# Second scores of one batch and first scores of the next in one run of matmuls, in shared banks

## The chip, the core and the metric

The kernel runs on one core of a Trainium2 chip. A core has a matrix engine (TensorE, in the profile PE, with its weight loads as PEld), three engines for the rest (VectorE or DVE, ScalarE or ACT, GpSimd or POOL), and queues that start transfers between the chip's main memory and the on-chip memory (SP and POOL start nearly all of them here). Matmuls write to eight accumulator banks (PSUM) of 128 partitions x 512 fp32 columns; DVE and ACT read them out. Every engine works through its own list of instructions in order, and waits on counters that other engines raise. The metric is the device time of one execution, in microseconds; before the change it is 241.86 us (median of 3 runs, 241.26 to 241.97).

## The reference

Eight batches, eight heads, 576 positions, head dimension 64, 32 "packed" queries `p` for each head. First attention: the packed queries attend to the keys. Second attention: the 576 queries attend to the 32 packed results, which are keys and values at once. Then a feed-forward layer with a squared relu on the 4608 positions.

```python
def sm_attn(qq, kk, vv):
    s = scale * np.matmul(qq, kk.transpose(0, 1, 3, 2))
    s = s - np.max(s, axis=-1, keepdims=True)
    a = np.exp(s)
    a = a / (np.sum(a, axis=-1, keepdims=True) + 1e-09)
    return np.matmul(a, vv)
p_packed = sm_attn(p, k, v)
out = sm_attn(q, p_packed, p_packed)
x = out.transpose(0, 2, 1, 3).reshape(B * S, H * D)
h = x @ w_in
r = np.maximum(h, 0.0)
return ((r * r) @ w_out).astype(np.float32)   # w_in 512 x 2048, w_out 2048 x 512
```

## The kernel before

Matmul operands are bf16, accumulators fp32. The eight heads of a batch are two "quads" of four (`NQ` is 2, `QH` is 4); all work of a batch `b` is done for quad 0 and quad 1.

The work is a list of words in the string `ORDER`, written out by hand or by a planner outside of the file. `run` walks through it and `step` turns each word into a few instructions. Every engine gets its instructions in the order of the words; a suffix (`:v`, `:a`, `:p`) says which engine does the word. There is no other scheduler: the words' order is the order in each queue, and waits are put in where one instruction needs another's data or its buffer. The words, with batch `b` and quad `i`:

- `Lk`, `Lv`, `Lq`, `Pr`: transfers of `k`, `v`, `q` and the packed queries, started by POOL, with a cast to bf16. `kTbi`, `qTbi`: transposition on DVE.
- `s1b` (both quads): the first scores, `p` against `k`. They contract over 64, in two steps `e` of 32, so one matmul uses a 32 x 32 corner of the array, and 16 of them run side by side. For batches 2 to 7 (`WIDE`) the packed queries are there twice, in `pT` and shifted by half the partitions in `pT1`, so both halves of the 576 columns (`HALVES`) can run at once, on tiles whose rows are turned by two. One quad's scores fill 288 columns in each of two banks.
- `m1`, `x1`: negated maximum (DVE), exponential with the sum (ACT). `eT`, `eo`: transposition of it by TensorE, eviction. `rd`, `pv`, `pp`: the product with `v` and its division. `bd`, `bs`: the packed result turned for the second scores, once as it is and once shifted (`ppd`, `ppd1`). `pt`, `po`: the same turned for the weights.
- `w0`, `w1`, evicted by `W0`, `W1`: the packed result is multiplied into `w_in` first (`st_wp`), since the second attention's values go only through it. These matmuls use 64 x 32 corners of the array.
- `s2b`: the second scores, `ppd` against `qT`, again 32 x 32 and 288 columns in each of two banks. `t2`: DVE transposes them out of the banks; `m2`, `sb`, `x2`, `su`, `a2`, `aT`: the softmax over 32 and the turned result.
- `hb.hf.fb`: one block of the first layer, 128 x 128, two matmuls of 288 columns, one a quad. `r`: relu out of the bank. `q`: the square of two blocks into `gT`.
- `ott.j`: two of the 16 matmuls (128 x 128, 512 columns) of output tile `tt`; `c` copies the tile out of its bank, `d` starts its transfer on SP.

Banks: `psa` has two double banks, taken in turn by `turn32` and `turn16` (lines 328 to 332) for the scores, `eT`, `pv`, `pt` and `w`; the pool `x` has two single banks for the output tiles, `y` two for the first layer. Output copies have five buffers, `k` three, `q` two. A quad's banks of `psa` come free when the last reader of its scores is done; an `h` needs the bank that the relu of the second `h` before it has read.

The order interleaves: while TensorE runs the dense `o` and `h` of one batch, DVE and ACT prepare the next. Around the change it runs `s1` of batch `b+1`, with its exponentials and `pv`, then `s2` of the same batch `b+1`, and so on; both are separate runs in the dense work, `s13 ... s23 ... s14 ... s24`.

Of the kernel before, what the change touches and what calls it, by code (L numbers as in the profile page):

```python
# [11 lines left out]
F32 = mybir.dt.float32  # L12
# [29 lines left out]

EARLY = 4
# [25 lines left out]
h1.0.11 o4.3 r1.0.11:v x121 h1.1.7 kT31 h1.0.15 eT20 Lq3 q1.0.5:a o4.4 r1.0.15:v eT21 r1.1.7:v q1.0.7:a o5.5 rd2 eo20:v
eo21:a h1.0.13 h1.1.2 r1.0.13:v o4.5 r1.1.2:v q1.0.6:a h1.1.6 pv2 r1.1.6:v h1.1.8 pp2 h1.1.0 q1.1.1:a r1.1.8:v Lk30 o5.6  # L70
qT21 q1.1.3:a o4.6 h1.1.12 r1.1.0:a bd2 pt2 qT20 o4.7 bs2:a Lk40 h1.1.5 po2:v r1.1.12:a o5.7 q1.1.0:v c4:a h1.1.10
r1.1.5:v c5:a s22 d4 r1.1.10:v h1.1.4 o6.0 t221 r1.1.4:a h1.1.9 d5 o7.0 q1.1.2:a t220 h1.1.13 r1.1.9:a o6.1 qT30
r1.1.13:a Lq4 h1.1.11 q1.1.4:a m221 w120 w121 r1.1.11:a o6.2 m220 W121:a h1.1.14 h1.1.15 W120:v Lv31 o6.3 r1.1.14:a
q1.1.6:a o7.1 o6.4 sb21:v r1.1.15:a Lv40 o7.2 q1.1.5:a kT30 o7.3 q1.1.7:a o7.4 sb20:v Lk41 x221 o6.5 qT31 o7.5 x220 o6.6
su21 o6.7 o7.6 su20 c6:a o7.7 w020 a221:v c7:a d6 w021 o8.0 W020:a a220:v o8.1 d7 o8.2 aT21 W021:a o8.3 aT20 o8.4 Lq5
h2.0.1 h2.0.0 r2.0.1:v o8.5 r2.0.0:a o8.6 q2.0.0:v h2.0.2 h2.0.3 r2.0.2:v o9.0 Lk50 o8.7 r2.0.3:v h2.0.5 c8:a s13
q2.0.1:v r2.0.5:a h2.0.4 d8 m130 o10.0 r2.0.4:a h2.0.6 kT40 h2.0.7 r2.0.6:a o10.1 r2.0.7:a q2.0.2:v h2.0.10 Lk51 x130
m131 o9.1 h2.0.8 r2.0.10:a q2.0.3:v o9.2 r2.0.8:a kT41 h2.0.13 x131 eT30 h2.0.9 r2.0.13:v o10.2 eo30:a rd3 r2.0.9:v
h2.1.1 eT31 q2.0.4:v h2.0.14 r2.1.1:a o10.3 r2.0.14:v eo31:a h2.0.11 Lk61 o9.3 r2.0.11:v o9.4 h2.0.12 h2.1.5 q2.0.5:v
r2.0.12:a pv3 r2.1.5:v h2.0.15 q2.0.6:v h2.1.4 pp3 r2.0.15:a o9.5 r2.1.4:v h2.1.6 bd3 pt3 q2.0.7:v h2.1.0 bs3:a o9.6  # L80
r2.1.6:v r2.1.0:v Lv41 po3:a o9.7 q2.1.2:v h2.1.8 q2.1.0:v c9:a h2.1.2 r2.1.8:v s23 r2.1.2:a Lv50 d9 o11.0 t230 h2.1.3
h2.1.7 t231 o10.4 r2.1.3:a w130 m230 r2.1.7:a w030 W130:a h2.1.10 q2.1.1:v h2.1.9 q2.1.3:v o10.5 W030:a m231 o10.6 o11.1
sb30:v r2.1.10:a o11.2 r2.1.9:a sb31:v o10.7 x230 o11.3 q2.1.4:v c10:a h2.1.15 qT40 o11.4 x231 h2.1.11 su30 r2.1.15:a
w031 d10 r2.1.11:a w131 W031:a h2.1.14 su31 h2.1.13 o12.0 r2.1.14:a a230:v o12.1 r2.1.13:a o12.2 W131:a q2.1.5:v o12.3
a231:v h2.1.12 o11.5 aT30 r2.1.12:a o12.4 aT31 o12.5 q2.1.6:v q2.1.7:v h3.0.5 h3.0.2 qT41 r3.0.5:a o12.6 h3.0.0 r3.0.2:v
Lq6 o11.6 r3.0.0:a o12.7 h3.0.1 h3.1.1 r3.0.1:v c12:a o11.7 r3.1.1:v s14 d12 c11:a q3.0.0:v h3.0.4 kT50 h3.0.3 r3.0.4:a
o13.0 r3.0.3:a m140 d11 h3.0.9 Lk60 o14.0 r3.0.9:a q3.0.1:v h3.1.3 x140 kT51 h3.1.0 o14.1 r3.1.3:a m141 o13.1 Lk70
r3.1.0:a h3.0.8 q3.0.2:v eT40 x141 h3.0.7 r3.0.8:v o13.2 eo40:v r3.0.7:a h3.0.6 q3.1.0:v o14.2 q3.0.4:v r3.0.6:a eT41
# [20 lines left out]
r5.1.0:a o23.0 bd6 pt6 r5.0.11:v h5.0.13 bs6:a o22.1 po6:v r5.0.13:v o23.1 q5.0.5:v o22.2 h5.0.15 o23.2 o22.3 r5.0.15:v
h5.1.1 h5.1.4 r5.1.1:v w061 w060 r5.1.4:v W061:a h5.0.14 q5.1.0:v o23.3 r5.0.14:v h5.0.12 W060:a o22.4 q5.0.7:v o22.5  # L110
r5.0.12:v h5.1.5 q5.0.6:v h5.1.2 o23.4 r5.1.5:v o22.6 r5.1.2:v h5.1.6 q5.1.2:v o22.7 r5.1.6:a h5.1.9 h5.1.3 c22:v s26
r5.1.3:a r5.1.9:a o23.5 t261 d22 o24.0 q5.1.1:v h5.1.11 h5.1.7 t260 r5.1.11:a o24.1 r5.1.7:a h5.1.12 m261 w161 r5.1.12:a
w160 m260 W161:a h5.1.8 o23.6 q5.1.3:v h5.1.15 r5.1.8:a sb60:v o24.2 W160:a o23.7 sb61:v h5.1.13 r5.1.15:a o24.3
q5.1.4:v x260 qT71 h5.1.10 s17 r5.1.13:a c23:a su60 o24.4 r5.1.10:a h5.1.14 d23 x261 o25.0 q5.1.6:v o25.1 q5.1.5:v
r5.1.14:a su61 o25.2 o24.5 q5.1.7:v o24.6 a260:v o25.3 o24.7 a261:v o25.4 aT60 o25.5 aT61 c24:a o25.6 m170 h6.0.1
h6.0.10 r6.0.1:a m171 o25.7 d24 x170 h6.0.4 r6.0.10:v o26.0 c25:a r6.0.4:v o26.1 qT70 x171 h6.0.0 h6.0.2 d25 o26.2
r6.0.0:v r6.0.2:a rd7 eT70 q6.0.0:v h6.0.14 eo70:v h6.0.9 r6.0.14:a o26.3 r6.0.9:v h6.0.5 o27.0 r6.0.5:v h6.0.6 eT71
q6.0.2:v r6.0.6:a h6.0.11 o26.4 eo71:v r6.0.11:a h6.0.3 q6.0.5:v h6.1.1 pv7 r6.1.1:v o26.5 r6.0.3:a pp7 o26.6 q6.0.1:v
# [19 lines left out]
class Kernel:  # L138
# [101 lines left out]
    def p_rest(self, word, engine):  # L240
# [621 lines left out]
```

## Time and profile before

| | |
|---|---|
| median of 3 runs | 241.86 us (241.26 to 241.97) |
| profiled execution | 242.64 us, span 240.8 us |
| TensorE busy | 228.9 us, 95% of the span, clock granted 1.0 |
| VectorE, ScalarE, GpSimd busy | 201.4, 144.2, 73.4 us |
| second layer (`ps_o`, L683) | 140.9 us summed over its records |
| first layer (`ps_h`, L625) | 89.9 us summed over its records |

The span is what the profiler saw of the core's work; the time of an execution contains some 1.8 us more around it. Matmuls overlap: a record of 512 columns lasts 379 ns but the next begins after some 216, so the pace is read from the starts of successive rows. A few matmul records are missing (2373 matmuls beside 2408 weight loads). In rows of the timeline stand start, length, engine, line, operation, output<-inputs, and how many were merged; a bracket gives the idle time before and what ended it. In grouped rows stand count, busy time, mean ns of one, and the idle time before.

### The profile page before, as it was taken

The page shows a single profiled execution, that of the slowest core. Times are in us where ns is not written, and L with a number is a line of the kernel's source. Part 1 is how long each engine was busy: PE and PEld are TensorE (multiplying, and loading weights), DVE is VectorE, ACT ScalarE, POOL GpSimd, SP SyncE. Part 2 cuts the span into 40 slices and gives each one's busy share as a digit, 9 for nine tenths or more (in the row PEclk, how much of TensorE's full clock was granted, in tenths as well). Part 3 has the DMA queues.
Part 4 walks back from the last instruction along what each step waited for, and adds up shares of the span by engine and source line. Part 5 has one row for each costly group of instructions (what it writes and reads, how often), then busy time and mean ns, then how long its engine had stood idle before and what let it go on. Part 6 is the DMA issues. An engine that isn't in the chain of part 4 may idle for free.

```text
span 240.8 us, 6042 instructions
## 1 busy us (share of the span) xinstructions
PE 228.9 (95%) x2373; PEld 124.6 (52%) x2408; DVE 201.4 (84%) x456; ACT 144.2 (60%) x311; POOL 73.4 (30%) x122
## 2 busy tenths in 40 slices
PE   8768999999999999999999999999999999999994
PEld 2444563456544564456555654465545644565543
DVE  2759986989998889989998889997899879987650
ACT  2247984787797657865693647774495346733300
POOL 8518782676583662054303340002000000000000
PEclk9999999999999999999999999999999999999999
DMA  6999999999999999159933993216113211112124
GB/s 108 177 197 209 187 197 206 172 239 195 197 194 211 177 169 144 44 78 211 110 79 37 196 125 52 59 37 102 39 23 73 49 46 44 44 41 49 46 63 112
DMA packets 33404, 28.51 MB, mean 118 GB/s; under 512 B 8160, under 2 KB 28384, under 8 KB 33376
## 3 DMA queue, kind: packets, MB, share of 16 engines
q0 software_dynamic: 26848, 18.55, 54.5%
q1 hardware_dynamic: 6384, 9.51, 14.7%
q8 instruction: 19, 0.31, 0.5%
q10 hardware_dynamic: 144, 0.07, 0.1%
q14 instruction: 9, 0.07, 0.1%
HBM read 37.22 MB, written 9.44 MB: 194 GB/s over the span
## 4 chain that ended last, share of the span: by engine, by line
PE 83%; DVE 7%; DMA 4%; issue 2%; POOL 1%; SPq 1%; ACT 1%; POOLq 0%
PE ps_o L683 48%; PE ps_h L625 25%; DMA gT<-in_v_dram 4%; PE ps_wp L609 3%; PE ps_s L408 3%; PE ps_e1T L466 2%; PE ps_pv L490 1%; SPq L714 1%; DMA out_dram<-o_sb 1%; DVE gT L670 1%; DVE mx L558 1%; DVE d L564 1%; DVE r L632 1%; DVE sums L576 1%; ACT qT L452 1%
## 5 line engine op out<-in xcount | busy, mean ns | idle before, releaser
L683 PE MATMUL ps_o<-w_out_bf,gT 128*128 128x512 bf16 (+1 forms) x544 | 140.9, 378 | 2.0 <-issue 0.5
L625 PE MATMUL ps_h<-a2T,wp 128*128 128x288 bf16 (+2 forms) x512 | 89.9, 286 | 1.4 <-DVE wp L454 0.6
L630 ACT ACTIVATE r<-ps_h 128x288 bf16<-128x288 f32 (+2 forms) x161 | 61.4, 413 | 48.8 <-PE ps_h L625 43.2
L683 PEld LDWEIGHTS <-gT 128*128 128x128 bf16 x576 | 54.6, 98 | 43.6 <-issue 3.4
L625 PEld LDWEIGHTS <-wp 128*128 128x128 bf16 x512 | 47.4, 98 | 41.9 <-issue 7.4
L632 DVE TENSOR_SCALAR r<-ps_h 128x288 bf16<-128x288 f32 (+2 forms) x95 | 41.3, 449 | 11.3 <-PE ps_h L625 10.6
L670 DVE TENSOR_TENSOR gT<-r 128x576 bf16<-128x576 bf16 (+2 forms) x108 | 46.5, 444 | 2.1 <-ACT r L630 1.2
L452 ACT CAST wp<-ps_wp 128x1024 bf16<-128x1024 f32 (+1 forms) x31 | 29.1, 962 | 8.8 <-PE ps_wp L609 8.8
L452 ACT COPY o_sb<-ps_o 128x512 f32<-128x512 f32 x26 | 15.2, 590 | 12.3 <-PE ps_o L683 12.0
L271 POOL DMA_DIRECT2D q_b<-in_q_dram x16 | 11.0, 690 | 27.4 <-DVE qT L366 25.4
L271 POOL DMA_DIRECT2D k_b<-in_k_dram x28 | 15.2, 545 | 13.5 <-DVE kT L354 4.6
L316 POOL DMA_DIRECT2D v_b<-in_v_dram x12 | 9.3, 776 | 31.8 <-PE ps_pv L490 29.8
L446 ACT ACTIVATE e<-ps_s,nm 128x576 bf16<-128x576 f32 x16 | 11.8, 742 | 7.1 <-DVE nm L434 6.8
L354 DVE STREAM_TRANSPOSE kT<-k_b 128x576 uint32<-128x576 uint32 x16 | 12.3, 771 | 3.1 <-DMA k_b<-in_k_dram 3.1
L668 ACT ACTIVATE gT<-r 128x640 bf16<-128x640 bf16 (+1 forms) x18 | 12.2, 695 | 0.4 <-DVE r L632 0.3
L434 DVE TENSOR_REDUCE nm<-ps_s 128x1 f32<-128x576 f32 x16 | 11.5, 739 | 1.0 <-PE ps_s L408 0.9
L366 DVE STREAM_TRANSPOSE qT<-q_b 128x576 uint32<-128x576 uint32 (+2 forms) x16 | 10.8, 683 | 1.8 <-DMA q_b<-in_q_dram 1.8
L576 DVE TENSOR_REDUCE sums<-e 128x18 f32<-128x576 f32 (+2 forms) x20 | 12.1, 603 | 0.0
L570 ACT ACTIVATE e<-d 128x576 f32<-128x576 f32 (+2 forms) x20 | 11.7, 600 | 0.7 <-DVE d L564 0.6
L564 DVE TENSOR_TENSOR d<-s,mx 128x576 f32<-128x576 f32 (+2 forms) x19 | 11.7, 641 | 0.0
L558 DVE TENSOR_REDUCE mx<-s 128x18 f32<-128x576 f32 (+2 forms) x20 | 11.6, 609 | 0.0
L584 DVE TENSOR_TENSOR a<-e,rs 128x576 bf16<-128x576 f32 (+2 forms) x17 | 11.6, 708 | 0.0
(66 smaller groups left out, 177.1 us busy)
## 6 DMA issues: line engine op xcount, KB each, us to landing
out_dram<-o_sb SPq DMA_DIRECT2D x65, 128.0 KB, 3.3
v_b<-in_v_dram POOLq DMA_DIRECT2D x12, 256.0 KB, 5.5
w_out_bf<-in_moe_w_out_dram POOLq DMA_DIRECT2D x4, 512.0 KB, 11.1
q_b<-in_q_dram POOLq DMA_DIRECT2D x6, 288.0 KB, 6.7
q_b<-in_q_dram POOLq DMA_DIRECT2D x12, 144.0 KB, 7.1
k_b<-in_k_dram POOLq DMA_DIRECT2D x12, 108.0 KB, 5.1
gT<-in_v_dram POOLq DMA_DIRECT2D x4, 288.0 KB, 8.5
w_in_bf<-in_moe_w_in_dram POOLq DMA_DIRECT2D x4, 256.0 KB, 11.4
```

What stands on the lines that cost most here:

```text
L271: engine.dma_start(x[n:], s[:P - n])
L354: self.nc.vector.transpose(t["kT"][:].rearrange("p s e -> p (s e)").bitcast(U32), t["k"][:].rearrange("p t d -> p (t d)").bitcast(U32))
L452: engine.copy(out, x)
L558: self.nc.vector.tensor_reduce(out=mx[:, x], in_=t["s2"][:, x], op=ALU.max, axis=AX.X)
L564: engine.tensor_tensor(out=d2[:, x], in0=t["s2"][:, x], in1=t["mx"][:, x].unsqueeze(2).to_broadcast([P, n, NP]), op=ALU.subtract)
L576: nc.vector.reduce_sum(out=sums[:, x], in_=t["e2"][:, x], axis=AX.X)
L625: self.nc.tensor.matmul(ps, lhsT=t["wp"][:, fb // n, fb % n * P:(fb % n + 1) * P], rhs=t["a2T"][:, s0:s1], start=(qd == 0), stop=(qd == se ...
L630: engine.activation(r, ps, ACT.Relu)
L632: engine.tensor_scalar_max(r, ps, 0.0)
L668: engine.activation(out, r, ACT.Square)
L670: engine.tensor_tensor(out=out, in0=r, in1=r, op=ALU.mult)
L683: self.nc.tensor.matmul(self.o[tt][:, e], lhsT=self.gT[:, fb, a:a + P], rhs=self.w_out_bf[:, fb, e], start=(i == 0), stop=(i == self.NFB - 1))
```

## The change

For batches 2 to 6 (`JOINED`) the second scores of batch `b` move into one run with the first scores of batch `b+1`: a word `Mb` (`st_join`) takes the place of `s2b` and `s1(b+1)`. The first scores of a quad leave 224 of the 512 columns free in each of its two banks. The first 224 and the last 224 of the 576 columns of second scores go there (`MAIN` is 7 of 18 groups of 32). The 128 in the middle go to a bank of the pool `y`, one a quad, so that both banks of the first layer are taken for the run. The run has 80 small matmuls instead of 2 x 32: first scores, then the two outer pieces, then the middle one. `s12` and `s27` stay as they were.

The transposition out of the banks becomes two words: `tX` for the 128 columns in the middle, `t2` for the two outer pieces. The quads' rows of `k` and `p` are turned the other way in quad 1 (`turned`), so that first and second scores go through the array's corners in the same order; their loads and that of `q` (`JOINED_CUTS`, 11 and 7 of 18 groups instead of 9 and 9) are cut to match.

`ORDER` is the same up to the word `o2.6` (272 words) and is laid out anew behind it. Counted behind that point: squares 61 on DVE and 51 on ACT (before 99 and 13), relus 66 and 158 (85 and 139), `W` 5 and 19 (2 and 22), `c` 10 and 23 (9 and 24); `w` stands in ten pairs and four single words (twelve pairs); output tiles and transfers stand in another order.

```diff
+JOINED = range(2, 7)
+MAIN = 512 // NP - T // 2
+JOINED_CUTS = (slice(0, T - MAIN), slice(T - MAIN, T))
...
+r1.1.12:a o5.4 M2 m131 o5.5 o5.6 tX21 t221 o4.7 tX20 q1.1.1:a o5.7 q1.1.2:a x131 d1 c4:a h1.1.10 t220 c5:a h1.1.11 w020 m221 ... o6.0
...
+M3 o8.7 m140 tX31 m141 q2.1.6:a q2.0.5:a o9.1 Lq5 tX30 o9.2 t230 c8:a h2.1.7 o10.0 t231 m230 o10.1 Lq4 h2.1.15 x140 Lv41 w030 x141 o10.2
+r2.1.15:a m231 sb30:v r2.1.7:a h2.1.5
...
+M4 o12.5 q3.0.0:a o11.7 tX41 tX40 c11:a t240 h3.1.0 h3.1.13 o12.6 r3.1.13:a o12.7 t241 m151 r3.1.0:a h3.1.5 h3.1.4
...
+M5 q4.0.3:a o17.0 o15.5 m161 tX51 tX50 Lk71 t251 m160 x161 t250 h4.0.15 h4.1.13 o17.1 m251 o17.2 m250 r4.1.13:a h4.1.10
...
+M6 o20.4 o21.4 m170 o20.5 tX60 tX61 q5.0.6:a o21.5 h5.1.10 o21.6 x170 t260 m171 t261 o21.7 m260 h5.1.7 x171 m261 q5.0.2:v o20.6 Lv71 eT71
...
-        cuts = WIDE_CUTS if b in WIDE else (self.span(hf),)
+        cuts = JOINED_CUTS if b in JOINED else WIDE_CUTS if b in WIDE else (self.span(hf),)
...
+    def turned(self, b, qd):
+        return (QH - qd) % QH if b in WIDE else qd if b else 0
...
+    def st_join(self, b):
+        x, y, z = [], [], []
+        for qd in range(self.NQ):
+            t, u = self.att[b, qd], self.att[b + 1, qd]
+            ps = u["ps_s1"] = self.turn32("ps_m")
+            t["ps_s2", 0], t["ps_s2", 1] = ps[:, :, HALF:], self.bank("y", "ps_s2")[:, :(T - 2 * MAIN) * NP].unsqueeze(1)
+            x.append((ps, [p[:, (b + 1) * self.NQ + qd, :] for p in (self.pT, self.pT1)], u["kT"],
+                      [((h + self.turned(b + 1, qd)) % QH, h) for h in range(QH)]))
+            tiles = [(h, self.group(qd, h)) for h in range(QH)]
+            y.append((t["ps_s2", 0], t["ppd"], t["qT"], tiles))
+            z.append((t["ps_s2", 1], t["ppd"], t["qT"], tiles))
+        m = MAIN * NP
+        self.scores(HALVES, x)
+        self.scores(((0, m), (S - m, S)), y)
+        self.scores(((m, S - m),), z)
+
+    def st_turnJ(self, t, extra):
+        s2 = self.new(t, self.tp, "s2", [P, 2 * (T - MAIN), NP], F32)
+        if extra:
+            self.nc.vector.transpose(s2[:, MAIN:T - MAIN].rearrange("p t i -> p (t i)"), t["ps_s2", 1][:, 0])
+        else:
+            self.nc.vector.transpose(s2[:].rearrange("p (a t) i -> p a t i", a=2)[:, :, :MAIN].rearrange("p a t i -> p a (t i)"),
+                                     t["ps_s2", 0])
```

More of the change, by code (lines that the diff above doesn't have):

```diff
@@ L69 @@
[L69 to L73, printed above, removed]
@@ L79 @@
[L79 to L83, printed above, removed]
@@ L84 @@
[L84 to L88, printed above, removed]
@@ L109 @@
[L109 to L113, printed above, removed]
@@ L114 @@
[L114 to L118, printed above, removed]
@@ new lines @@
+q2.0.7:v h2.0.12 r2.0.13:a r2.0.12:a po3:a o8.5 h2.1.13 r2.1.13:a h2.0.10 o9.0 kT41 h2.1.2 bs3:v Lv40 r2.0.10:a h2.1.0
+q2.0.6:a kT40 o8.6 qT31 r2.1.0:v r2.1.2:a M3 o8.7 m140 tX31 m141 q2.1.6:a q2.0.5:a o9.1 Lq5 tX30 o9.2 t230 c8:a h2.1.7
+o10.0 t231 m230 o10.1 Lq4 h2.1.15 x140 Lv41 w030 x141 o10.2 r2.1.15:a m231 sb30:v r2.1.7:a h2.1.5 r2.1.5:a h2.1.4 o10.3
+o10.4 h2.1.11 o9.3 o10.5 sb31:v w131 W030:a x230 w031 r2.1.4:v q2.1.0:v o9.4 r2.1.11:a h2.1.8 x231 o10.6 h2.1.6 W131:a
+su30 r2.1.8:a w130 r2.1.6:a su31 d8 h2.1.14 r2.1.14:a W031:a o9.5 h2.1.9 a230:v o10.7 a231:v o9.6 c10:a d6 h2.1.10 aT30
@@ new lines @@
+o17.0 o15.5 m161 tX51 tX50 Lk71 t251 m160 x161 t250 h4.0.15 h4.1.13 o17.1 m251 o17.2 m250 r4.1.13:a h4.1.10 r4.0.15:a
+o17.3 h4.0.14 x160 r4.1.10:v w151 w051 d9 o15.6 sb50:v q4.0.5:v o17.4 Lv61 h4.1.12 r4.0.14:a W151:a o15.7 r4.1.12:v
+o17.5 W051:a c15:a h4.1.5 x250 q4.1.5:v d13 h4.1.0 o17.6 r4.1.0:a w150 w050 h4.1.7 o18.0 sb51:v x251 r4.1.5:v W050:a
+su50 r4.1.7:a o18.1 h4.1.4 o17.7 h4.1.6 eT60 r4.1.4:a a250:v r4.1.6:a su51 h4.1.1 o18.2 eo60:v o18.3 r4.1.1:a c17:a
+h4.1.8 a251:v rd6 q4.0.6:a h4.1.9 r4.1.8:a eT61 o19.0 aT51 o19.1 q4.1.2:v d17 r4.1.9:a eo61:v h4.1.14 h4.1.15 o19.2 pv6
@@ new lines @@
+r5.1.5:a h5.0.5 r5.0.5:a h5.0.15 o21.3 d10 qT60 q5.0.5:v r5.0.15:a M6 o20.4 o21.4 m170 o20.5 tX60 tX61 q5.0.6:a o21.5
+h5.1.10 o21.6 x170 t260 m171 t261 o21.7 m260 h5.1.7 x171 m261 q5.0.2:v o20.6 Lv71 eT71 eT70 r5.1.7:a o20.7 d18 c21:a
+sb61:v rd7 q5.1.2:v h5.1.12 sb60:v r5.1.10:a c20:v h5.1.6 o22.0 eo70:a eo71:v r5.1.12:a o22.1 x261 o22.2 h5.1.11
+r5.1.6:a h5.1.13 x260 o22.3 r5.1.13:v w160 r5.1.11:a w161 q5.0.4:v h5.1.15 r5.1.15:a su61 h5.1.8 Lv70 q5.0.7:v su60
+a260:v o23.0 o23.1 q5.1.6:v W160:a r5.1.8:a q5.1.5:a o22.4 h5.1.1 o23.2 Lq7 a261:v pv7 h5.1.14 r5.1.14:a o23.3 o23.4
@@ L300, in load1 @@
             for hf, y in enumerate(WIDE_CUTS):
[L301 removed]
+                self.load_rows(x[:, y, :], s[:, y, :], (self.turned(b, qd) + 2 * hf) % QH)
         else:
@@ L417, in st_s1 @@
             p = [y[:, b * self.NQ + qd, :] for y in (self.pT, self.pT1)[:2 if b in WIDE else 1]]
-            x.append((t["ps_s1"], p, t["kT"], [((h + (qd if b else 0)) % QH, h) for h in range(QH)]))
+            x.append((t["ps_s1"], p, t["kT"], [((h + self.turned(b, qd)) % QH, h) for h in range(QH)]))
         self.scores(THIRDS if b in THREES else HALVES, x)
@@ L545, in st_turn2 @@
         nc = self.nc
-        s2 = self.new(t, self.tp, "s2", [P, T, NP], F32)
+        s2 = self.new(t, self.tp, "s2", [P, 2 * (T - MAIN), NP], F32)[:, :T]
         if pairs:
```

120 lines of the change are left out of this document (68 added, 52 removed).

## The prediction

> **What bounds the kernel now.** I read the page's totals first, then the chain that ended last, then the busy time of every engine in stretches.
>
> ```profile
> span 240.8 us, 6042 instructions
> PE 228.9 (95%) x2373; PEld 124.6 (52%) x2408; DVE 201.4 (84%) x456; ACT 144.2 (60%) x311; POOL 73.4 (30%) x122
> PE 83%; DVE 7%; DMA 4%; issue 2%; POOL 1%; SPq 1%; ACT 1%; POOLq 0%
> ```
> ```profile
> 60.00:90.00 30.00, 29.74 (x334) 16.16 (x338) 26.67 (x55) 22.20 (x47) 18.74 (x33) 1.00 1.15 191
> 120.00:150.00 30.00, 29.79 (x298) 16.18 (x300) 27.68 (x61) 18.96 (x41) 6.72 (x11) 1.00 0.59 98
> 180.00:210.00 30.00, 29.63 (x267) 16.25 (x271) 27.71 (x63) 16.28 (x36) 0.00 (x0) 1.00 0.23 54
> ```
>
> The columns of the second view are stretch, its length, PE, weight loads, DVE, ACT, POOL (busy us, instructions), granted clock, DMA share, GB/s. TensorE leaves 0.2 to 0.4 us in 30, at clock 1.00; VectorE is 89 to 92% busy beside it, ScalarE 54 to 74%. So from the first dense matmuls to the end TensorE has no wait left to remove: a gain must come from fewer microseconds of TensorE work, and any new wait in TensorE's queue is lost in full. The paces come from these rows (start, length, what, count):
>
> ```profile
> 226.69 0.49 PE ps_h L625 x4
> 229.64 2.60 PE ps_o L683 x12
> ```
> An `h` word (two matmuls of 288 columns) is 0.49/2 = 0.245 us, an `o` word (two of 512) 2.60/6 = 0.433 us.
>
> **The change part by part.** *The joined run on TensorE.* A separate score run and a `w` pair look like this:
>
> ```profile
> 55.07 0.38 PE L625 MATMUL ps_h<-a2T,wp 128*128 128x256 bf16 x2
> 55.39 0.48 PE L408 MATMUL ps_s<-kT,pT 32*32 32x288 bf16 x32
> 55.80 0.39 PE L625 MATMUL ps_h<-a2T,wp 128*128 128x256 bf16 x2
> 67.65 0.43 PE L625 MATMUL ps_h<-a2T,wp 128*128 128x320 bf16 x2
> 68.01 0.62 PE L609 MATMUL ps_wp<-w_in_bf,ppT 64*32 64x512 bf16 x16
> 68.57 0.61 PE L683 MATMUL ps_o<-w_out_bf,gT 128*128 128x512 bf16 x2
> ```
>
> Two matmuls of 256 columns stream 2 x 0.109 us (the pace of 288 scaled), so the first is due to hand over at 55.29; the next dense matmul starts at 55.80. A score run costs 0.51 us: two steps (the two halves of the head dimension, 16 tiles side by side) of 288 columns, 0.245, and 0.265 of changing shape. The joined run has six steps: two of 288 (0.245), two of 224 (0.19), two of 128 (0.11), plus one 0.265: 0.81. Five joined runs replace ten: 5 x (1.02 - 0.81) = 1.05 us saved. The columns now fall in three pieces and 16 more small matmuls a run are issued (80 more in all); that costs nothing as long as the steps follow one another as the two do now; without that cover each of the four added steps could cost a tenth, and the saving is gone. *The split `w` runs.* A pair costs 68.57 - (67.65 + 0.27) = 0.65, of which 0.433 streams and 0.22 is shape change. The new order has 10 pairs and four single `w`s where there were 12 pairs: two more runs, 0.43 us. Nine more alternations of `h` and `o`, of which the rows resolve no more than 0.02 each, I take as 0.05 (0 to 0.2). Net on TensorE: -1.05 + 0.43 + 0.05 = about **-0.6 us** (bounds -1.05, if a single `w` costs only its stream, and 0).
>
> *VectorE and ScalarE.* The rows for the moved instructions, and for those behind a joined run:
>
> ```profile
> L630 ACT ACTIVATE r<-ps_h 128x288 bf16<-128x288 f32 x121 | 46.9, 414 | 45.1 <-PE ps_h L625 39.9 <-issue 1.8 <-DVE qT L366 1.5
> L670 DVE TENSOR_TENSOR gT<-r 128x576 bf16<-128x576 bf16 x96 | 41.5, 446 | 2.1 <-ACT r L630 1.2
> L632 DVE TENSOR_SCALAR r<-ps_h 128x288 bf16<-128x288 f32 x71 | 30.8, 448 | 9.9 <-PE ps_h L625 9.3
> L452 ACT CAST wp<-ps_wp 128x1024 bf16<-128x1024 f32 x27 | 26.9, 1019 | 7.5 <-PE ps_wp L609 7.5
> L452 ACT COPY o_sb<-ps_o 128x512 f32<-128x512 f32 x26 | 15.2, 590 | 12.3 <-PE ps_o L683 12.0 <-DMA out_dram<-o_sb 0.3
> L446 ACT ACTIVATE e<-ps_s,nm 128x576 bf16<-128x576 f32 x16 | 11.8, 742 | 7.1 <-DVE nm L434 6.8
> L434 DVE TENSOR_REDUCE nm<-ps_s 128x1 f32<-128x576 f32 x16 | 11.5, 739 | 1.0 <-PE ps_s L408 0.9
> L550 DVE STREAM_TRANSPOSE s<-ps_s 128x576 f32<-128x576 f32 x12 | 8.8, 761 | 0.9 <-PE ps_s L408 0.9
> L668 ACT ACTIVATE gT<-r 128x640 bf16<-128x640 bf16 x10 | 7.2, 747 | 0.0
> L668 ACT ACTIVATE gT<-r 128x512 bf16<-128x512 bf16 x8 | 5.0, 630 | 0.4 <-DVE r L632 0.3
> L454 DVE CAST wp<-ps_wp 128x1024 bf16<-128x1024 f32 x3 | 3.7, 1218 | 0.4 <-PE ps_wp L609 0.4
> L553 DVE STREAM_TRANSPOSE s<-ps_s 128x320 f32<-128x320 f32 x2 | 1.0, 494 | 0.0
> ```
>
> Counted in the two orders, 38 squares and 19 relus leave VectorE for ScalarE, three `W` evictions and one `c` go the other way. A transposition has 0.761 us at 576 columns and 0.494 at 320, so 1.04 ns a column: 0.63 for 448 and 0.29 for 128, together 0.16 more than one of 576, ten times. VectorE: -38 x 0.446 - 19 x 0.448 + 3 x 1.218 + 0.7 + 1.6 = -19.5 us. ScalarE: +38 x 0.69 (between its 512 and 640) + 19 x 0.414 - 3 x 1.019 - 0.6 = +30 us, to about 175 of 241, 73%. In sum neither becomes the bound; and as TensorE never waited for VectorE, the 19.5 us buy nothing by themselves.
>
> *What waits behind a joined run.* In the new program one pair of banks holds both kinds of scores, and the waits that it was built with keep their readers apart: the maximum of the first scores waits until the second scores in its bank are written; ScalarE's exponential waits for VectorE's transposition wherever that stands ahead in the order; after M6 a transposition waits for an exponential. A bank of either pool comes free only after all three. Behind the waiting exponential, in ScalarE's queue, stand relus that free the two banks of the first layer. I walk the stretch after each joined run with TensorE's paces and these rows; instructions on one engine overlap a little:
>
> ```profile
> 55.91 1.42 DVE L434 TENSOR_REDUCE nm<-ps_s 128x1 f32<-128x576 f32 x2 [0.23 <-PE ps_s L408]
> 65.71 1.45 DVE L550 STREAM_TRANSPOSE s<-ps_s 128x576 f32<-128x576 f32 x2
> 132.17 0.71 ACT L630 ACTIVATE r<-ps_h 128x288 bf16<-128x288 f32 x2 [0.79 <-PE ps_h L625]
> 133.83 0.73 ACT L446 ACTIVATE e<-ps_s,nm 128x576 bf16<-128x576 f32 x1
> 134.45 0.20 ACT L446 ACTIVATION_READ_ACCUMULATOR e<-ps_s,nm 128x1 f32 x1
> 134.54 0.74 ACT L446 ACTIVATE e<-ps_s,nm 128x576 bf16<-128x576 f32 x1
> ```
>
> So a maximum holds VectorE about 0.66 and ends after 0.74, a transposition holds it 0.07 less than its length, an exponential holds ScalarE 0.71, a relu 0.30; a hand-over I take as 0.04. With 0 at the end of the joined run:
> - M3: maximum 0 to 0.74, tX31 to 0.94, second maximum to 1.61, tX30 to 1.81, t230 to 2.37, exponential x140 2.4 to 3.15. TensorE has five `o` and two `h` words (2.66) plus the shape change 0.1 before w030, which needs that bank: wait 0.4. Then x141 to 3.85, its accumulator read, relu r2.1.15 to about 4.25; h2.1.5, due at 3.96, needs the relu's bank: 0.35.
> - M5: h4.0.15 is due at 0.87, tX51 ends at 0.94: 0.1. t251 ends at 1.72, x161 at 2.5, relu r4.1.13 at 2.9; h4.1.10 is due at 2.33: 0.6.
> - M6: maximum to 0.74, x170 to 1.52, only then t260 to 2.19, second maximum to 2.86, t261 to 3.4, x171 to 4.18. eT71, which transposes x171's output, is due at 3.52 (seven `o`, two `h`): 0.7.
> - M2: x131 after t221 ends at 2.28, then c4 to 2.85; o6.0 needs its bank and is due at 2.70: 0.15, and h2.0.7, whose inputs pass the whole softmax, perhaps 0.2.
> - M4: readers ahead of every bank's next use: none.
>
> Together 2.3 to 2.5 us; I take **+2.4**. The bounds are 0, if these readers go faster than their rows, and about 5, if ScalarE comes late to each.
>
> [...]
>
> *Loads and stores.* POOL's queue keeps its number of issues; the `q` loads are cut 11 and 7 rows instead of 9 and 9, and quadrant 1 of `k` and `p` is turned the other way, with the same bytes.
>
> ```profile
> POOL q_b L271 <- DVE qT L366: 25.4, 2, 13.1
> k_b<-in_k_dram POOLq DMA_DIRECT2D x12, 108.0 KB, 5.1
> q_b<-in_q_dram POOLq DMA_DIRECT2D x12, 144.0 KB, 7.1
> out_dram<-o_sb SPq DMA_DIRECT2D x65, 128.0 KB, 3.3
> ```
> POOL's issues wait long for buffers now, so loads run ahead. In the new order I count at least 9 us of TensorE work between a `k` issue and its use (31) and 14 for `q`, against 5.1 and 7.1 to land: nothing, but if the first is late, the run that follows waits with it. SP passes some `d`s far back, but takes them in turn as soon as their `c` is done; an output buffer is still wanted again 7 us later at the earliest, against 3.3. The last `c` and `d`s end before the last tile's copies. Nothing.
>
> The sum: -0.6 + 2.4 = +1.8 us. The profiled execution took 242.64 (span 240.8 and 1.8 around it), 0.8 above the median of 241.86; on that median I predict **243.7 us**. A measurement of this kernel can tell about 0.3%, 0.7 us, from no change.
>
> **The rivals.** *The waits are hidden (other side).* One mechanism: the readers behind the joined runs, M3, M5 and M6 above all, clear the banks before TensorE's list comes to them. Price: none of the 2.4, so -0.6, 241.3; with the single `w`s free, 240.8. It decides if the first exponential after M3 ends within 2.8 us of the run and r4.1.13 after M5 within 2.3. For it: VectorE has 19.5 us less to do, and its idle shares today show no wait of TensorE. Against: the chains contain only instructions of the join itself, and each is a row above. *ScalarE becomes the bound.* Squares stand between relus, and two banks feed every `h`. If a tenth of ScalarE's added 30 us reaches TensorE, 3 us come on top of the forecast: 246.7. For it: the relus already are the longest waits of ScalarE, so they are served the moment they come, which a queue three quarters full no longer does. Between M3 and M4 ScalarE's rows add up to 23 us against TensorE's 22. Against: with the overlap above (a relu holds 0.30 of its 0.414) they are about 19. *The joining saves nothing* (steps don't follow closely): +1.05 on the forecast, 244.8; it lies inside the forecast's range.
>
> **How the numbers follow.** Forecast with waits of 1 to 4 us: 0.52, own range 242.3 to 245.3. ScalarE as bound: 0.18. Waits hidden: 0.30, of which 0.12 reaches -0.7 us and 0.18 lies within 0.3%. So faster 0.12, same 0.18, slower 0.70. The range takes in most of both rivals: 241.0 to 247.0.
>
> **What the profile after would show.** Right: TensorE idle behind score runs of batches 3, 5 and 6, released by ACT (exponential, relu) and DVE; score runs of about 0.8 us; DVE near 182, ACT near 175 us busy; TensorE 29.0 to 29.5 of 30 in the middle. Wrong: no idle there (first rival); idle spread over all `h` with ACT as releaser (second); joined runs of 1 us or more (third); idle with DMA as releaser would overturn my reading of the loads.

## The result, and the profile after

The changed kernel takes 245.47 us (median of 4 runs, 245.38 to 245.9) where the kernel before took 241.56 in the runs made beside it: 1.0166 times as long (95% interval 1.0141 to 1.0191), 3.9 us slower. The profiled execution took 245.38, its span is 243.6.

The totals and the chain that ended last, from the page of the changed kernel:

```profile
span 243.6 us, 6259 instructions
PE 232.5 (95%) x2488; PEld 127.2 (52%) x2488; DVE 185.9 (76%) x417; ACT 167.2 (69%) x360; POOL 73.4 (30%) x122
PE 84%; DVE 7%; ACT 3%; DMA 2%; issue 1%; POOL 0%; ACTq 0%; POOLq 0%
```

VectorE went from 201.4 to 185.9 us and ScalarE from 144.2 to 167.2. The forecast was 182 and 175: the direction is right, but ScalarE gained 23 us and not 30. TensorE still fills 95% of a longer span.

The timeline around M3, TensorE's rows with the readers of the joined run (columns: start, length, engine, line, operation, what it writes and reads, size, count, and in brackets the idle time before and what ended it):

```profile
86.16 0.59 PE L721 MATMUL ps_o<-w_out_bf,gT 128*128 128x512 bf16 x2
86.68 0.48 PE L420 MATMUL ps_m<-kT,pT 32*32 32x288 bf16 x32
87.01 0.53 PE L420 MATMUL ps_m<-qT,ppd 32*32 32x224 bf16 x32
87.29 0.36 PE L420 MATMUL ps_s<-qT,ppd 32*32 32x128 bf16 x16
87.59 1.47 PE L721 MATMUL ps_o<-w_out_bf,gT 128*128 128x512 bf16 x6
89.28 1.14 DVE L466 STREAM_TRANSPOSE s<-ps_m 128x448 f32<-128x448 f32 x2
89.92 0.74 ACT L484 ACTIVATE e<-ps_m,nm 128x576 bf16<-128x576 f32 x1 [1.10 <-DVE s L466]
90.80 0.41 PE L647 MATMUL ps_wp<-w_in_bf,ppT 64*32 64x512 bf16 x8 [0.39 <-ACT e L484]
91.14 0.60 PE L721 MATMUL ps_o<-w_out_bf,gT 128*128 128x512 bf16 x2
```

Two things stand here. The joined run costs 1.00 us, not 0.81: the two output matmuls that start at 86.16 have streamed by 86.59 (one `o` word, 0.433), and the next dense matmul starts at 87.59. Its three pieces start 0.33, 0.28 and 0.30 apart. And ScalarE stands idle for 1.10 us before the exponential, until a transposition that reads the same bank is done, so that TensorE stands idle before `w030`, which needs that bank. Behind M5 and M6 the same chain:

```profile
138.28 0.74 ACT L484 ACTIVATE e<-ps_m,nm 128x576 bf16<-128x576 f32 x1 [1.47 <-DVE s L466]
139.46 0.41 PE L663 MATMUL ps_h<-a2T,wp 128*128 128x288 bf16 x2 [0.44 <-ACT r L668]
...
166.68 0.65 DVE L466 STREAM_TRANSPOSE s<-ps_m 128x448 f32<-128x448 f32 x1 [0.48 <-ACT e L484]
168.62 0.74 ACT L484 ACTIVATE e<-ps_m,nm 128x576 bf16<-128x576 f32 x1 [1.97 <-DVE s L466]
169.50 0.75 PE L504 MATMUL ps_e1T<-ident,e 128*128 128x128 bf16 x10 [0.72 <-ACT e L484]
```

Not all of the last 1.97 us belongs to the transposition right ahead of that exponential. The maximum that it needs ends only at 167.97, because it stands on VectorE behind the transposition of 166.68, which waited for the exponential before.

In two places of the same timeline that are not behind a joined run, TensorE loses time too:

```profile
54.34 0.77 DVE L363 STREAM_TRANSPOSE kT<-k_b 128x576 uint32<-128x576 uint32 x1
54.91 0.71 PE L420 MATMUL ps_s<-kT,pT 32*32 32x288 bf16 x32
...
81.55 0.68 ACT L706 ACTIVATE gT<-r 128x576 bf16<-128x576 bf16 x1
81.96 0.59 PE L721 MATMUL ps_o<-w_out_bf,gT 128*128 128x512 bf16 x2
82.25 0.46 DVE L670 TENSOR_SCALAR r<-ps_h 128x288 bf16<-128x288 f32 x1 [0.47 <-PE ps_h L663]
82.76 0.41 PE L663 MATMUL ps_h<-a2T,wp 128*128 128x288 bf16 x2 [0.20 <-DVE r L670]
```

The separate run `s12` lasts 0.71 where its like take 0.48: a transposition of `k` ends at 55.11, within it, and holds its second half back by 0.2. At 82.76 an `h` word starts 0.37 late (81.96 and 0.433 make 82.39), for a bank that the relu of 82.25 on VectorE (`r2.0.14`) had not read. That relu writes into a buffer that the square of 81.55 on ScalarE (`q2.0.4`) still reads until 82.23; before the change this square was on VectorE.

From the starts of successive rows over the whole dense stretch (from the first unbroken run of output tiles to the last tile), the two profiled executions differ by 4.0 us. (Their spans differ by 2.8 only, because in the profile before that stretch begins at 43.05, 1.1 us later than the 41.91 of the one after.) Worked out word by word, each run against its stream and against its like before:

| part | predicted | in the trace |
|---|---|---|
| joining: 5 runs of 1.00 for 10 of 0.51 | -1.05 | -0.1 |
| two more `w` runs | +0.43 | +0.5 |
| alternations of `h` and `o` | +0.05 | not resolved |
| waits behind M2, M3, M5, M6 | +2.4 | +2.6 (0.2, 0.7, 0.75, 0.9) |
| the remainder: waits elsewhere | 0 | +1.0 |
| sum | +1.8 | +4.0 |

The shares of M2 are 0.23 at `w020`, of M3 0.46 at `w030` and 0.26 at `h2.1.5`, of M5 0.60 at `h4.1.10` and 0.15 at `h4.0.15`, of M6 0.88 at `eT71`; M4 has none, as forecast. The remainder is what is left of the 4.0. It has 0.37 before M3, 0.2 at `s12` and 0.2 at the first transposition of batch 2; the others are 0.2 or less each.

### The profile page after: what moved, and what is told of

The parts are those of the page before. It is cut to its first block, busy times and chain, and to the rows that moved or that the text cites. A ratio compares the mean times of both kernels' runs of the same rounds, so it can differ in the third digit from the quotient of the medians.

```text
span 243.6 us, 6259 instructions
## 1 busy us (share of the span) xinstructions
PE 232.5 (95%) x2488; PEld 127.2 (52%) x2488; DVE 185.9 (76%) x417; ACT 167.2 (69%) x360; POOL 73.4 (30%) x122
## 4 chain that ended last, share of the span: by engine, by line
PE 84%; DVE 7%; ACT 3%; DMA 2%; issue 1%; POOL 0%; ACTq 0%; POOLq 0%
PE ps_o L721 47%; PE ps_h L663 25%; PE ps_wp L647 3%; DMA k_b<-in_k_dram 2%; DVE nm L472 2%; PE ps_e1T L504 2%; ACT e L484 2%; PE ps_m L420 2%; PE ps_pv L528 1%; PE ps_s L420 1%; DVE s L466 1%; DVE sums L614 1%; ACT qT L490 1%; DVE s L464 0%; PE ps_ppT L567 0%
## 5 line engine op out<-in xcount | busy, mean ns | idle before, releaser
L721 PE MATMUL ps_o<-w_out_bf,gT 128*128 128x512 bf16 (+1 forms) x576 | 148.3, 378 | 0.1
L668 ACT ACTIVATE r<-ps_h 128x288 bf16<-128x288 f32 (+2 forms) x180 | 69.5, 415 | 40.5 <-PE ps_h L663 39.4
L670 DVE TENSOR_SCALAR r<-ps_h 128x288 bf16<-128x288 f32 (+2 forms) x76 | 33.7, 452 | 24.8 <-PE ps_h L663 23.8
L706 ACT ACTIVATE gT<-r 128x576 bf16<-128x576 bf16 (+2 forms) x56 | 37.6, 687 | 2.4 <-DVE r L670 2.1
L490 ACT CAST wp<-ps_wp 128x1024 bf16<-128x1024 f32 (+1 forms) x28 | 26.4, 958 | 5.2 <-PE ps_wp L647 5.2
L708 DVE TENSOR_TENSOR gT<-r 128x576 bf16<-128x576 bf16 (+2 forms) x70 | 29.6, 438 | 0.4 <-ACT r L668 0.2
L275 POOL DMA_DIRECT2D k_b<-in_k_dram x28 | 15.4, 553 | 26.4 <-DVE kT L363 15.1
L490 ACT COPY o_sb<-ps_o 128x512 f32<-128x512 f32 x25 | 14.5, 587 | 4.3 <-PE ps_o L721 3.8
L647 PE MATMUL ps_wp<-w_in_bf,ppT 64*32 64x512 bf16 (+1 forms) x272 | 11.1, 370 | 1.0 <-ACT e L484 0.4
L277 POOL DMA_DIRECT2D k_b<-in_k_dram x19 | 9.9, 523 | 6.4 <-DMA v_b<-in_v_dram 3.2
L484 ACT ACTIVATE e<-ps_m,nm 128x576 bf16<-128x576 f32 x10 | 7.4, 744 | 6.3 <-DVE s L466 5.5
```

Of the source, the lines that this page charges most:

```text
L275: engine.dma_start(x[n:], s[:P - n])
L484: self.nc.scalar.activation(out, x, ACT.Exp, bias=t["nm"], accum_out=self.den[b][:, qd:qd + 1])
L490: engine.copy(out, x)
L647: self.nc.tensor.matmul(ps[NP * g:NP * g + NP, c, :f1 - f0], lhsT=t["ppT"][D * c:D * c + D, NP * h:NP * h + NP], rhs=self.w_in_bf[D * c:D ...
L668: engine.activation(r, ps, ACT.Relu)
L670: engine.tensor_scalar_max(r, ps, 0.0)
```

## The experiments

The times of the kernel before that the ratios refer to were taken on the same chip as each experiment: 241.53, 241.58 and 241.38 us. Line numbers in the experiments differ by one or more from those of the two kernels.

**Exponentials first.** Theory: TensorE waits behind M3, M5 and M6 because an exponential stands behind a transposition. The edit moves the exponentials ahead, and with them some maxima and relus that stood behind; M5 as an example:

```diff
-M5 q4.0.3:a o17.0 o15.5 m161 tX51 tX50 Lk71 t251 m160 x161 t250 h4.0.15 h4.1.13 o17.1 m251 o17.2 m250 r4.1.13:a h4.1.10 r4.0.15:a
-o17.3 h4.0.14 x160
+M5 q4.0.3:a o17.0 o15.5 m161 tX51 tX50 Lk71 x161 m160 h4.0.15 h4.1.13 t251 o17.1 r4.1.13:a m251 o17.2 h4.1.10 r4.0.15:a x160 o17.3
+t250 h4.0.14 m250
```

> The changed kernel with some 20 words behind M3, M5 and M6 in another order, so that the exponentials of the first scores stand ahead of the transpositions of the second ones (before, they waited for them); nothing is added or left out. Theory (TensorE loses about 2.2 us behind these three joined runs because an exponential waits for a transposition in the same bank): the three stalls seen in the trace of the changed kernel, 0.46 and 0.26 behind M3, 0.61 behind M5, 0.88 behind M6, go, and the time falls from 245.5 by 1.6 to 2.3 us, to 243.2 to 243.9. Rival (ScalarE is the bound, or the stalls only move): less than 0.6 us.

243.81 us (243.66 to 244.07), ratio 1.0092 (1.0076 to 1.0108): 1.66 us off, within the theory's range. The total of ScalarE's waits for that transposition, from the view of who waited for whom (columns: in total, times, longest), in the changed kernel:

```profile
ACT e L484 <- DVE s L466: 5.5, 4, 2.0
```

and in the reordered one:

```profile
ACT e L485 <- DVE s L467: 0.9, 1, 0.9
```

In its timeline `w030` and `eT71` behind M6 start without a wait:

```profile
90.30 0.41 PE L664 MATMUL ps_h<-a2T,wp 128*128 128x288 bf16 x2
90.64 0.41 PE L648 MATMUL ps_wp<-w_in_bf,ppT 64*32 64x512 bf16 x8
...
167.71 0.59 PE L722 MATMUL ps_o<-w_out_bf,gT 128*128 128x512 bf16 x2
168.15 0.72 PE L505 MATMUL ps_e1T<-ident,e 128*128 128x128 bf16 x10
```

Of the 2.2 us of these stalls all but 0.5 came back as time. The 0.5 are new stalls: 0.28 at the `w` pair behind M5, whose bank now waits for the later transposition, and 0.25 at 99.05 us, where an `h` waits for relus that stand behind VectorE's transpositions.

**Split `w` pairs in the kernel before.** For all twelve pairs of batches 2 to 7:

```diff
-w130 m230 r2.1.7:a w030 W130:a h2.1.10
+w130 m230 r2.1.7:a W130:a h2.1.10 w030
```

> The kernel before, with the second word of each of its twelve w pairs of batches 2 to 7 moved behind the next dense word, so that there are 24 single w runs where there were 12 pairs. Theory (each separate run of small matmuls pays for changing the array's shape): 12 x 0.21 = 2.5 us slower than before, 244.1 (2.0 to 3.0 more). Rival (a single w costs only its stream): no change, 241.6.

244.18 us, ratio 1.0112 (1.0098 to 1.0126): 2.65 us slower, 0.22 for each added run. In its timeline a single `w` takes 0.34 to the next dense matmul, and 0.10 ahead of it (92.16 and 0.433 make 92.59):

```profile
92.16 0.59 PE L684 MATMUL ps_o<-w_out_bf,gT 128*128 128x512 bf16 x2
92.69 0.41 PE L610 MATMUL ps_wp<-w_in_bf,ppT 64*32 64x512 bf16 x8
93.03 0.42 PE L626 MATMUL ps_h<-a2T,wp 128*128 128x288 bf16 x2
```

So 0.44 for a single one, against 0.65 for a pair: the term of the prediction holds.

**The joined run cut in two.** In the changed kernel, for M2 to M6 (N is the second part; M4 is shown):

```diff
-o11.6 bd4 bs4:a r3.1.1:a r3.0.12:v q3.0.3:a M4 o12.5
+M4 o11.6 bd4 bs4:a r3.1.1:a r3.0.12:v q3.0.3:a N4 o12.5
```

> The changed kernel with each joined run cut in two: the first scores are issued one o word earlier, that o word runs, then the second scores follow; the same instructions, five more changes of shape. By the prediction (a change of shape costs 0.265 us): 5 x 0.265 = 1.3 us slower than the changed kernel, 246.8. By the trace of the changed kernel (the fixed cost sits in the steps, 0.05 each, and a change of shape costs 0.17): 5 x 0.17 = 0.85 us slower, 246.3. If changing shape costs nothing: 245.5.

247.02 us (246.46 to 248.16), ratio 1.0231 (1.021 to 1.0253), 1.55 slower than the changed kernel. But in the profiled execution, the slowest of the five, one wait is new, at M2, where the first part comes before the last transposition of its `k` is done; from its timeline, with the cut run M3 below:

```profile
61.60 0.78 DVE L364 STREAM_TRANSPOSE kT<-k_b 128x576 uint32<-128x576 uint32 x1 [1.50 <-DMA k_b<-in_k_dram]
...
64.84 0.45 PE L421 MATMUL ps_m<-kT,pT 32*32 32x288 bf16 x24 [0.58 <-DVE kT L364]
...
88.30 0.47 PE L421 MATMUL ps_m<-kT,pT 32*32 32x288 bf16 x32
88.70 0.60 PE L728 MATMUL ps_o<-w_out_bf,gT 128*128 128x512 bf16 x2
89.24 0.43 PE L421 MATMUL ps_m<-qT,ppd 32*32 32x224 bf16 x32
89.54 0.35 PE L421 MATMUL ps_s<-qT,ppd 32*32 32x128 bf16 x16
89.82 1.47 PE L728 MATMUL ps_o<-w_out_bf,gT 128*128 128x512 bf16 x6
```

A load of `k` was late in this execution: VectorE waited 1.50 us for it, where it waits 0.28 in the changed kernel. So most of the wait at M2 is the load's. (In the changed kernel the transposition in question ends at 63.07, and a first part one `o` word ahead of 63.38 would wait for it 0.1 us, by estimate.) With times from 1.0 to 2.7 us above the changed kernel, the five cuts cost 0.2 to 0.5 each, and the times don't tell 0.18 from 0.265. The rows do: the parts take 0.40 and 0.58 and 0.10 ahead of each, together 1.18 for 1.00, and M4, M5 and M6 show the same to 0.01. A change of shape there and back costs 0.18, and not the 0.265 that the prediction took.

**Without the middle piece.** The third piece of every joined run is left out, so the second scores of 128 columns are not computed:

```diff
-            t["ps_s2", 0], t["ps_s2", 1] = ps[:, :, HALF:], self.bank("y", "ps_s2")[:, :(T - 2 * MAIN) * NP].unsqueeze(1)
+            t["ps_s2", 0], t["ps_s2", 1] = ps[:, :, HALF:], ps[:, :1, HALF:HALF + (T - 2 * MAIN) * NP]
-            z.append((t["ps_s2", 1], t["ppd"], t["qT"], tiles))
-        self.scores(((m, S - m),), z)
```

> The changed kernel without the third piece of the joined run: the 32 small matmuls on the 128 columns in the middle (two steps of 16) are left out in all five runs, tX reads 128 of the other columns instead, no bank of the first layer is taken; so the second scores of those columns are not computed. By columns alone (the prediction's term for them, 0.11 a run): 0.55 us faster than the changed kernel, 244.9, and some 0.15 more because h4.0.15 no longer waits for a bank. If each step also costs a fixed 0.05 us: 5 x (0.11 + 0.10) = 1.05, 244.4, with the bank 244.3. If it is the hand-over to another bank that is slow (0.3 a run for the piece): 1.5, 244.0.

246.24 us (245.66 to 248.21), ratio 1.0206 (1.0177 to 1.0235): not faster at all, against everything expected. (The piece is 16 matmuls a run, as the rows of the joined run show, and not the 32 of the expectation.) The timeline of the fastest of its executions, at M3 and at the stalls behind M3, M5 and M6:

```profile
86.71 0.48 PE L421 MATMUL ps_m<-kT,pT 32*32 32x288 bf16 x32
87.04 0.53 PE L421 MATMUL ps_m<-qT,ppd 32*32 32x224 bf16 x32
87.50 1.47 PE L720 MATMUL ps_o<-w_out_bf,gT 128*128 128x512 bf16 x6
...
90.83 0.41 PE L646 MATMUL ps_wp<-w_in_bf,ppT 64*32 64x512 bf16 x8 [0.51 <-ACT e L483]
...
139.37 0.41 PE L662 MATMUL ps_h<-a2T,wp 128*128 128x288 bf16 x2 [0.71 <-ACT r L667]
...
166.00 0.74 ACT L483 ACTIVATE e<-ps_m,nm 128x576 bf16<-128x576 f32 x1 [1.13 <-DVE s L463]
...
169.70 0.75 PE L503 MATMUL ps_e1T<-ident,e 128*128 128x128 bf16 x10 [1.13 <-ACT e L483]
```

The run itself is shorter by 0.12 (0.79 from its start to the next dense matmul, 0.91 with the piece), as the columns alone say (0.11). But the three stalls grew from 0.39, 0.44 and 0.72 to 0.51, 0.71 and 1.13, by 0.8 in all. From the start of the joined run to the word that waits it is 4.12 us behind M3 and 3.88 behind M5 in both kernels (86.68 to 90.80 and 86.71 to 90.83; 135.58 to 139.46 and 135.49 to 139.37). So there the pace is not TensorE's: what TensorE saves it waits longer, at M3 the 0.12, at M5 the 0.12 and the 0.15 that `h4.0.15` no longer waits. Behind M6 the same stretch grew from 5.30 to 5.60, and that is the edit's own doing: `tX` now reads the shared bank, so the first exponential waits for it too and starts 1.90 after the run's start (164.10), where the changed kernel has 1.61 (164.20):

```profile
165.81 0.74 ACT L484 ACTIVATE e<-ps_m,nm 128x576 bf16<-128x576 f32 x1 [0.84 <-DVE nm L472]
```

The experiment therefore shows what paces these stretches, but its time is no price of the piece alone, and why its executions lie 2.5 us apart is open.

**Twice as many small matmuls, the same columns.** In the kernel before, the twelve separate runs of batches 2 to 7, with `m` a quarter of the columns:

```diff
+            for k in range(2):
+                for e in range(2):
...
+                                self.nc.tensor.matmul(ps[c, hf, k * m:k * m + m], ...
+                                                      rhs=y[r, s0:s0 + m, e], start=(e == 0), stop=(e == 1))
```

> The kernel before; in its twelve separate score runs of batches 2 to 7 every small matmul of 288 columns is cut into two of 144, so a run has 64 small matmuls instead of 32, with the same columns and the same results. By the prediction's price (a run costs its columns and one change of shape): no change, 241.6. By the trace of the changed kernel (its small matmuls of 224 columns start every 8.3 ns, whatever they stream): 32 more of 8.3 to 10.4 ns in each of 12 runs, 3.2 to 4.0 us slower, 244.7 to 245.5.

244.59 us, ratio 1.0125 (1.011 to 1.014): 3.0 us slower, with not one column more. The timeline, at `s13`:

```profile
79.63 0.41 PE L640 MATMUL ps_h<-a2T,wp 128*128 128x288 bf16 x2
79.97 0.75 PE L411 MATMUL ps_s<-kT,pT 32*32 32x144 bf16 x64
80.65 0.42 PE L640 MATMUL ps_h<-a2T,wp 128*128 128x288 bf16 x2
```

0.68 from the run to the next dense matmul, where the separate run shown in the prediction takes 0.41. 32 more small matmuls are 0.27 us, 8.4 ns each.

**The load moved, the order kept.** In the kernel before, only suffixes change: 38 squares and 19 relus `:v` to `:a`, three `W` `:a` to `:v`.

> The kernel before, in its own order, with only the load moved as in the changed one: behind the word o2.6, 38 squares and 19 relus, evenly spaced, go from VectorE to ScalarE and three W evictions the other way. Theory (neither engine becomes the bound, TensorE does not wait for ScalarE): within 0.7 us of 241.5. Rival (ScalarE becomes the bound): a tenth of the 30 us comes through, 3 us slower, 244.5, with idle time of TensorE spread over the first layer's matmuls and released by ScalarE.

248.31 us, ratio 1.028 (1.0265 to 1.0296): 6.7 slower, more than either side expected. From the page and from the view of who waited for whom:

```profile
PE 230.7 (94%) x2373; PEld 124.5 (51%) x2408; DVE 185.7 (75%) x402; ACT 169.2 (69%) x365; POOL 73.4 (30%) x122
...
PE ps_h L626 <- ACT r L631: 1.8, 5, 0.6
PE ps_o L684 <- ACT gT L669: 1.2, 3, 0.5
```

ScalarE is hardly busier than in the changed kernel (169.2 and 167.2 us), yet TensorE now waits for its relus and squares. The two waits shown are 3.0 of the 6.7 us; where the rest lies is open. What it shows is that a sum of 69% is no proof that moved work is free: the same amount of it cost 6.7 us in one order and at most the remainder of 1.0 in the other.

**Three attempts at the other waits.** The first starts from the kernel with the exponentials first:

```diff
-M2 m131 o5.5 o5.6 tX21 t221 o4.7 tX20 q1.1.1:a o5.7 q1.1.2:a x131 d1 c4:a h1.1.10 t220
+M2 m131 o5.5 x131 o5.6 tX21 tX20 o4.7 t221 q1.1.1:a o5.7 t220 q1.1.2:a d1 c4:a h1.1.10
...
-q2.0.0:v h2.0.15 q2.0.4:a r2.0.14:v
+r2.0.14:v h2.0.15 q2.0.4:a q2.0.0:v
```

> The reordered changed kernel of the first experiment, with the exponential put ahead of the transpositions behind M2 too, one word of cover more ahead of h4.0.15 and the transposition t250 ahead of a maximum behind M5, and the relu r2.0.14 ahead of a square before M3. Theory (what is left are waits of this kind, 0.32 behind M2, 0.36 before M3, 0.15 and 0.28 behind M5, read from the two traces): 0.8 to 1.1 us faster than the first experiment, 242.7 to 243.0. If they only move: 243.8.

245.09 us (244.53 to 246.35), ratio 1.0155 (1.0117 to 1.0192): 1.3 slower than without it. Behind M2 the two squares now stand ahead of the copy `c4`, and the output word that needs its bank waits:

```profile
67.91 1.46 PE L722 MATMUL ps_o<-w_out_bf,gT 128*128 128x512 bf16 x6 [0.60 <-ACT o_sb L491]
...
82.92 0.46 DVE L671 TENSOR_SCALAR r<-ps_h 128x288 bf16<-128x288 f32 x1 [0.85 <-ACT gT L707]
```

The second row settles the wait before M3. The relu `r2.0.14` now stands ahead of VectorE's square, and still does not start earlier: it waits for ScalarE's square, which holds its buffer, and the `h` behind it is 0.32 late as before (0.37).

The second attempt starts from the first one and takes the words from `o2.6` to the first transposition of batch 2 in the order of the kernel before.

> The same as the run before it, with the words from o2.6 up to the first transposition of batch 2 in the order of the kernel before, so that the separate score run s12 no longer stands right behind the transposition of k. Theory (the changed order loses 0.5 to 0.9 us between 48 and 60 us, 0.22 of it at s12): 242.0 to 242.5. Rival (what was late there becomes late at M2): 242.7 to 243.3. Nothing here should get below the kernel before by more than the 0.1 us that the joined runs save.

250.77 us, ratio 1.0374 (1.0349 to 1.0399). It says nothing on the waits, because in the mixed order a `kT` (`kT30`) stands only eight words behind its load, and TensorE waits behind VectorE:

```profile
65.83 0.78 DVE L364 STREAM_TRANSPOSE kT<-k_b 128x576 uint32<-128x576 uint32 x1 [4.03 <-DMA k_b<-in_k_dram]
```

The third starts from the kernel with the exponentials first again and makes six small shifts, each against one wait, for instance

```diff
-M2 m131 o5.5 o5.6 tX21 t221 o4.7 tX20 q1.1.1:a o5.7 q1.1.2:a x131 d1 c4:a h1.1.10 t220
+M2 m131 o5.5 o5.6 tX21 tX20 o4.7 x131 t221 d1 c4:a o5.7 q1.1.1:a q1.1.2:a h1.1.10 t220
```

> The kernel of the first experiment with six small shifts, each against one wait left in its trace: the last transposition of k ahead of two squares before s12 (0.2), one first-layer word more ahead of the first transposition of batch 2 (0.2), behind M2 the exponential x131 and the copy c4 ahead of two squares (0.23), one relu behind M3 on ScalarE ahead of a copy (0.25), and behind M5 one output word more ahead of h4.0.15 (0.15) and of the w pair (0.28). Theory (these waits are separate and each has room behind it): 1.0 to 1.3 us faster than the first experiment, 242.5 to 242.8; the rest to the kernel before is then the split w runs (0.5) and what is left around 49 and 82 us. Rival (they only move, as in the seventh run): 243.6 to 244.

244.46 us (244.2 to 244.48), ratio 1.0125 (1.0108 to 1.0142): 0.65 slower than without it. `s12` is at 0.50 again, now that its `kT` stands ahead of two squares on VectorE, and `w020` has lost its 0.23. But the wait at the first transposition of batch 2 only moved to the `h` word that was put ahead of it, which starts 0.33 late (57.06 and 0.22 make 57.28; it starts at 57.61, behind a relu on VectorE). And the evictions on ScalarE come later, so the next pair waits in its middle:

```profile
71.82 0.41 PE L648 MATMUL ps_wp<-w_in_bf,ppT 64*32 64x512 bf16 x8
72.79 0.41 PE L648 MATMUL ps_wp<-w_in_bf,ppT 64*32 64x512 bf16 x8 [0.56 <-ACT wp L491]
```

So two of these small waits went, and others moved along the two queues. None of the versions came below the kernel before, and the table says why: with every wait gone and the `w` pairs whole again, the joined runs would be worth 0.1 us (an estimate from its first row).

## Why the prediction was right, and where not

*Slower, and by which mechanism.* Right. The stalls are where the walk behind each joined run put them, in about the sizes that it gave: M3 0.72 (0.75), M5 0.75 (0.7), M6 0.88 (0.7), M2 0.23 (0.35), M4 none. The first exponential after M3 ends 3.07 us behind the run, where the walk had 3.15. The reorder of some 20 words took away three quarters of what the three stalls cost, which no other theory of this document explains; how much of that is the exponentials' and how much is that of the relus moved with them, it does not tell apart. In the trace the exponential waits for the transposition of other columns in its bank, 1.10, 1.47 and 1.97 us behind M3, M5 and M6; what a program without these waits would do, no run shows.

*The forecast of 243.7 was 1.8 too low; two terms failed.* The measured 245.47 lies just above the forecast's own range (242.3 to 245.3); it lies within 241.0 to 247.0, but that range takes in the rivals and is no close test. The first term that failed is the saving of the joined run, "0.245 and 0.265 of changing shape", and "that costs nothing as long as the steps follow one another as the two do now". The cover that the prediction named is not there: small matmuls cost more than their columns. In M3 the 32 of 288 columns start 0.33 us before the next piece, where their columns make 0.245; the 32 of 224 columns 0.28, where their columns make 0.19; and 32 more of 144, with no column more, cost 0.27 in the kernel before. The change of shape between them is 0.18 and not 0.265; the prediction had put into it what belongs to the matmuls. Two separate runs cost 1.02. Joined, they save one change of shape (0.18) and 0.05 (0.28 for 0.33), and pay 0.12 for the 16 in the middle, which would make 0.91. The trace has 1.00. The missing 0.09 lies on the way back to the dense matmuls: behind the 32 of 224 columns it takes 0.18 (in the run without the middle piece 0.46 to the next dense matmul, where M3 has 0.28 to the next small one), behind the first scores 0.08 (0.41 and 0.33). Why it is longer there, no run shows. The third rival (+1.05) described this, and its sign, joined runs of 1 us or more, came true; the prediction had called the condition for it by name, but took the cheap end.

*The second is the waits elsewhere, put at nothing.* The rows before M3 and at `s12` were never walked; only the stretches behind joined runs were. They are about 1.0 us. The load moved to ScalarE is shown as the cause of one, the 0.37 before M3: a square that used to be VectorE's holds the buffer of a relu. At `s12` it is the other way round: two squares that were ScalarE's before (`q1.0.7` and `q1.0.2`) now stand on VectorE ahead of a `kT`, and with the `kT` ahead of them the run was at 0.50 again. The cause of the others is open.

*The split pairs.* Right: 0.43 forecast, some 0.5 in the trace, and 0.22 a run where twelve were split.

*The rivals.* "Waits hidden" is out: the first exponential after M3 ended at 90.66, about 3 us after the run, and the bound was 2.8. "ScalarE becomes the bound" is out as the main cause, since reordering alone gave 1.66 us back at the same ScalarE load. But its argument was better than I made it: the same load in the old order cost 6.7 us, and the wait before M3 is of its kind. Of the signs named beforehand, TensorE's 29.0 to 29.5 us of 30 was too low for three of the four stretches between 60 and 180 us (29.70, 29.53, 29.56 and 29.28).

*Loads, stores and the tail.* As forecast they cost TensorE nothing behind the start; VectorE waited once for a load, 0.28 us for a `k` of batch 3, and M2, which needs it, was not late. In the slowest execution of the cut run that wait was 1.50 us, and there M2 was late by 0.58.

## What to carry to other kernels

Price a run of small matmuls by their number as well as by their columns (here 32 more at the same columns cost 0.27 us), and find the fixed part by doubling the number at the same columns, before counting on a saving from joining runs. When two results share a bank, list the readers of that bank in order on both engines: the one that a later step needs first should stand first, which here was worth 1.66 us for twenty words of order. A tuned order with no waits is one whole: moving work to an engine that is 60% busy, or healing waits by a shift of a few words, cost time in four of five tries here. Look also for waits that are not for a bank: the relu before M3 waited for a buffer that a moved square still read.

## What the runs showed of the hardware

- Small matmuls (32 x 32; in M3 80 weight loads for the 80 of them) cost 8.4 ns each at 144 columns (0.27 us for 32 more in a run) and 8.8 at 224 (0.28 for 32, in the middle of a run). They don't all start at one distance: the first 16 of M3 all start between 86.68 and 86.73, 3.3 ns apart, and the 32 of 224 columns behind them 8.3 ns apart, from 87.01 to 87.27.
- A change of shape from dense matmuls to 32 x 32 and back cost 0.18 us beyond the matmuls where a run was cut in two (0.10 ahead and 0.08 behind), to 64 x 32 and back 0.22 (2.65 for twelve more runs).
- Leaving out 16 small matmuls in each of five runs (0.12 us each) made nothing faster: behind M3 and M5 the readers of the banks set the pace, 4.12 and 3.88 us from the start of the run with the matmuls and without, and TensorE waited longer by what it saved.
